# Spatial mixing of a gMLP as seven block products (Strassen) in two sweeps, with the projection as a stage of its own

## The chip, the cores and the metric

The kernel runs on one core of a Trainium2 chip. The metric is the device time of one execution in microseconds (us). Each time given is a median over executions unless a profile is named.

## The reference

Attention (32 heads, the last 512 of 2048 cached positions) gives `s`; a gMLP gives a gate; the output joins them. Cut to what matters:

```python
x  = A_x                                    # 2048 x 512
xn = layernorm(x)
s  = attention(xn) @ wo                     # 2048 x 512
z  = gelu(xn @ w_in)                        # 2048 x 1376
z1 = z[:, :688]
z2 = layernorm(z[:, 688:])                  # 2048 x 688
g  = w_sp @ z2 + b_sp[:, None]              # spatial mixing: 2048x2048 by 2048x688
B  = (z1 * g) @ w_out                       # projection: 688 -> 512
out = x + s * silu(B)
```

Everything is f32.

## The kernel before

**Precision.** TensorE (PE) multiplies here in fp32r, a form of f32 with fewer bits. To keep f32 accuracy each operand is split in two: `hi`, a cast to fp32r on ScalarE (ACT), and `lo`, what is left (`rest`, line 59: `whole - hi`), on VectorE (DVE) or GpSimd (POOL). A product is then three matmuls, hi x hi, hi x lo and lo x hi (`mm3`, lines 65 to 67). So every operand costs an ACT cast and a subtraction before PE can use it.

**Stages.** The program is one instruction stream for each engine, in an order fixed when it is built; nothing is reordered on the chip.

1. *Attention* fills the first 1450 us. In its gaps the first half of z (`z1`, ahead of its gelu) is computed and stored in DRAM (`z1_dram`), and `s` ends up in `s_dram`.
2. *z* (lines 781 to 826): the 16 row tiles of the second half of z, in the order `ZO` (tiles 8 to 15, then 0 to 7). For each: two products of 344 columns into PSUM (`z_product`), gelu on ACT into `z` (`z_gelu`, line 789), statistics and norm on DVE (`z_norm`), and the split into `z2` hi and lo on ACT and POOL (`z_split`, line 807; the last tile's rest on DVE). `z2` then holds all of the normed z, as operands of the right side, 2 x 344 columns for each of 16 chunks of rows.
3. *Mixing and projection* (lines 832 to 994), a loop over the 16 row tiles `i` of `w_sp`:
   - `mix(i)`: 16 chunks x 2 column halves x 3 = 96 matmuls of 344 columns, into the two PSUM banks `ps_g0` and `ps_g1`.
   - `take(4)`: the next row tile of w_sp, in four pieces of 512 columns, is split (ACT cast, line 884; DVE rest), and further pieces of 256 KB are fetched eight pieces ahead on the queue of SyncE (SP).
   - `gate(i)` (line 906, DVE): `u = (g + b_sp) * gelu(z1)` from PSUM, in three instructions; the last 48 columns are written twice so that the projection's sixth chunk can hold hi and lo at once.
   - `send_u(i)`: u must stand transposed for the projection. DVE transposes its 32 x 32 blocks (line 913) into `uB`, and a store to DRAM (`u_dram`) with four loads back puts the blocks in place (`uL`). Only the last tile is transposed on PE (`flip_u`, line 935).
   - `split_u(i-1)` (cast, line 926; two rests on DVE) and `project(i-1)`: 17 matmuls of 512 columns into `ps_f`, silu on ACT, times `s` and plus `x` on DVE (lines 961, 962), and the store to `out`.

So one tile's projection runs behind the next tile's mixing, and the DRAM round trip of u and the splits of w_sp lie beside some 18 us of matmuls each time. The last two tiles are finished in pieces.

Memory: a ring of "x8" buffers, 8 KB per partition each, free after attention, holds w_sp's raw pieces and operands (in the profile all of them are `x`). PSUM has eight banks.

## Time and profile before

| | |
|---|---|
| median of 3 runs | 1812.49 us (1811.61 to 1812.63) |
| span of the profiled execution | 1813.9 us |
| DMA over the span | 394.08 MB, 217 GB/s |

Busy time of each engine by stage (us), in the profiled execution:

| from, to | stage | PE | DVE | ACT | POOL | GB/s |
|---|---|---|---|---|---|---|
| 0 to 1452.5 | attention | 1436.76 | 1242.09 | 1037.57 | 1199.47 | 236 |
| 1452.5 to 1511.5 | z | 59.00 | 34.33 | 26.72 | 33.00 | 67 |
| 1511.5 to 1801 | mixing, projection | 289.50 | 114.68 | 105.55 | 4.78 | 162 |
| 1801 to 1814 | the last tiles | 8.83 | 5.02 | 3.56 | 0.00 | 42 |

The profile is of one execution. A row of a group gives line, engine, operation, output and inputs by the program's names, tile size and count, then the busy time in us, the mean of one in ns, and the idle time ahead of the group with what ended it. A row of the timeline gives the start, the duration (of a group of like instructions, from the first's start to the last's end), the instruction and, in brackets, what it waited for. A row of the windows gives for each engine the busy us and, as x387, the number of instructions, then the granted TensorE clock, the busy share of the DMA engines and their GB/s. PEld is the loading of weights into PE, which overlaps with its matmuls.

### The profile page before, as it was taken

To read this page: it belongs to the slowest core of one execution; us is meant where nothing else is said; L and a number is where in the kernel's file an instruction comes from. 1 tells how busy PE (TensorE), PEld (TensorE's weight loads), DVE (VectorE), ACT (ScalarE), POOL (GpSimd) and SP (SyncE) were. 2 spreads that over 40 slices of the span, in tenths; PEclk is the share of its full clock that TensorE was granted. 3 is DMA by queue.
4 is the path that set the end of the run, shared out by engine and by line. 5 is a ranking of instruction groups with operands and counts; after the bars stand their busy time and mean duration, and the time that the engine had idled before them with its cause. 6 is when DMAs were issued, how large, how long until landed. Compare 5 with 4: busy or idle time off the path is not lost.

```text
span 1813.9 us, 28901 instructions
## 1 busy us (share of the span) xinstructions
PE 1794.1 (99%) x8658; PEld 1541.1 (85%) x8658; DVE 1396.1 (77%) x2369; ACT 1173.4 (65%) x2625; POOL 1237.3 (68%) x1179
## 2 busy tenths in 40 slices
PE   8999999999999999999999999999999999999999
PEld 7888888888888887788888888888888999999998
DVE  5689988989998988788888888888888556433333
ACT  3777777777777776577777777777776444433332
POOL 2798898898888987778888888888887343000000
PEclk8999999999999999999999999999999999999999
DMA  4688887988888989787777777777778725554532
GB/s 168 190 237 239 246 263 228 264 253 231 262 246 244 261 235 294 248 261 222 220 232 223 219 226 224 224 217 231 232 213 268 225 88 170 172 173 146 185 118 93
DMA packets 181805, 394.08 MB, mean 217 GB/s; under 512 B 24368, under 2 KB 54832, under 8 KB 164496
## 3 DMA queue, kind: packets, MB, share of 16 engines
q1 hardware_dynamic: 177040, 386.60, 71.7%
q10 hardware_dynamic: 4608, 5.64, 0.9%
q8 instruction: 68, 1.11, 0.2%
q14 instruction: 89, 0.73, 0.1%
HBM read 225.42 MB, written 166.72 MB: 216 GB/s over the span
## 4 chain that ended last, share of the span: by engine, by line
PE 91%; DVE 3%; DMA 3%; ACT 1%; issue 1%; POOL 1%; SPq 0%; ACTq 0%; DVEq 0%; POOLq 0%
PE ps_a L450 15%; PE ps L67 12%; PE ps L65 12%; PE ps L66 12%; PE ps_a L517 6%; PE ps_a L516 6%; PE ps_a L515 6%; PE ps_g L67 4%; PE ps_g L66 4%; PE ps_g L65 4%; PE ps_a L67 2%; PE ps_a L66 2%; PE ps_a L65 2%; DMA x<-x_dram 1%; PE ps_f L67 1%
## 5 line engine op out<-in xcount | busy, mean ns | idle before, releaser
L59 POOL TENSOR_TENSOR pT_l<-pL,pT_h 128x512 fp32r<-128x512 f32 x507 | 656.5, 1298 | 187.5 <-ACT pT_h L507 169.9
L479 ACT ACTIVATE prob<-ps,nm 128x512 f32<-128x512 f32 x512 | 353.9, 691 | 339.4 <-DVE nm L477 331.7
L539 DVE SCALAR_TENSOR_TENSOR sacc<-ps,sums,sacc 128x512 f32<-128x512 f32 x496 | 370.2, 747 | 128.5 <-PE ps L67 122.8
L450 PE MATMUL ps_a<-x,x 128*128 128x512 f32 x1302 | 376.4, 389 | 4.4 <-DMA x<-x_dram 4.4
L488 DVE STREAM_TRANSPOSE pL<-prob 128x512 f32<-128x512 f32 x512 | 359.2, 702 | 3.0 <-ACT prob L479 3.0
L477 DVE TENSOR_REDUCE nm<-ps 128x1 f32<-128x512 f32 x512 | 340.6, 665 | 6.6 <-PE ps L67 6.5
L507 ACT CAST pT_h<-pL 128x512 fp32r<-128x512 f32 x512 | 318.4, 622 | 20.1 <-DMA pL<-p_dram 7.0
L450 PEld LDWEIGHTS ps_a<-x,x 128*128 128x128 f32 x1302 | 244.5, 188 | 56.5 <-DMA x<-x_dram 4.8
L59 POOL TENSOR_TENSOR wl<-raw,wh 128x512 fp32r<-128x512 f32 x186 | 241.4, 1298 | 13.4 <-ACT wh L144 13.4
L517 PE MATMUL ps_a<-pT_l,wh 128*128 128x512 f32 x512 | 200.4, 391 | 2.0 <-POOL pT_l L59 1.8
L65 PE MATMUL ps<-wh,qT_h 128*128 128x512 f32 x512 | 199.9, 390 | 0.6 <-DVE sacc L539 0.6
L67 PE MATMUL ps<-wh,qT_l 128*128 128x512 f32 x512 | 200.0, 391 | 0.3
L515 PE MATMUL ps_a<-pT_h,wh 128*128 128x512 f32 x512 | 199.9, 391 | 0.0
L65 PE MATMUL ps<-wh,oT_h 128*128 128x512 f32 x512 | 199.7, 390 | 0.0
L66 PE MATMUL ps<-wl,qT_h 128*128 128x512 f32 x512 | 199.5, 390 | 0.0
L67 PE MATMUL ps<-wh,oT_l 128*128 128x512 f32 x512 | 199.5, 390 | 0.0
L516 PE MATMUL ps_a<-pT_h,wl 128*128 128x512 f32 x512 | 199.5, 390 | 0.0
L66 PE MATMUL ps<-wl,oT_h 128*128 128x512 f32 x512 | 199.5, 390 | 0.0
L67 PE MATMUL ps_g<-z_h,x 128*128 128x344 f32 x512 | 161.8, 316 | 0.0
L65 PE MATMUL ps_g<-z_h,x 128*128 128x344 f32 x512 | 161.8, 316 | 0.0
L66 PE MATMUL ps_g<-z_l,x 128*128 128x344 f32 x512 | 161.8, 316 | 0.0
L59 POOL TENSOR_TENSOR x<-wq,x 128x256 fp32r<-128x256 f32 x186 | 138.1, 743 | 1.5 <-ACT x L432 1.5
(197 smaller groups left out, 3184.9 us busy)
## 6 DMA issues: line engine op xcount, KB each, us to landing
p_dram<-pL SPq DMA_DIRECT2D x128, 1024.0 KB, 4.8
pL<-p_dram SPq DMA_DIRECT2D x256, 192.0 KB, 4.0
raw<-wh SPq DMA_DIRECT2D x188, 256.0 KB, 6.2
pL<-p_dram SPq DMA_DIRECT2D x256, 128.0 KB, 4.0
pL<-p_dram SPq DMA_DIRECT2D x256, 64.0 KB, 4.0
wq<-wh SPq DMA_DIRECT2D x62, 256.0 KB, 5.6
x<-w_sp SPq DMA_DIRECT2D x60, 256.0 KB, 5.8
x_dram<-rawx SPq DMA_DIRECT2D x32, 256.0 KB, 5.8
```

The lines of the kernel that those rows point to most:

```text
L59: engine.tensor_tensor(lo, whole, hi.bitcast(F32), op=OP.subtract)
L65: nc.tensor.matmul(ps, lh, rh, start=first, stop=False)
L66: nc.tensor.matmul(ps, lh, rl, start=False, stop=False)
L67: nc.tensor.matmul(ps, ll, rh, start=False, stop=last)
L450: nc.tensor.matmul(qps[g, bank], wt["q", g, k][a][:, c * P:(c + 1) * P], X[g * 2 // H][ORDER[k]][:, b, c], start=first, stop=r == 5, skip_ ...
L477: nc.vector.tensor_reduce(nm, ps, axis=AX.X, op=OP.max, negate=True)
L479: nc.scalar.activation(prob[t], ps, AF.Exp, bias=nm, accum_out=sums[b][:, j:j + 1])
L488: nc.vector.transpose(pL[b][:, :, j * P:j * P + P].rearrange("p a (c q) -> p a c q", q=Q), prob.pop(t).rearrange("p (a c q) -> p a c q", a ...
L507: nc.scalar.copy(h, p)
L515: nc.tensor.matmul(pps[b], vh, ph, start=c == 0, stop=False)
L517: nc.tensor.matmul(pps[b], vh, pl, start=False, stop=c == 3)
L539: nc.vector.scalar_tensor_tensor(at, ps, rs, at, op0=OP.mult, op1=OP.add)
```

## The change

The mixing is the only part whose arithmetic is changed; attention and the products of z stay, and so do the 272 matmuls of the projection.

**Seven products.** w_sp is cut into row tile pairs `r` (tiles r and r + 8) and two halves of its columns, and z into row halves and column halves (344 each). So for a pair there are blocks a11, a12, a21, a22 (128 x 1024 each) and b11, b12, b21, b22. The plain way needs eight block products for a pair; Strassen's scheme, in Winograd's form, needs seven, of sums of blocks:

```
S1 = a21 + a22   S3 = a11 - a21   S2 = S1 - a11   S4 = a12 - S2
T1 = b12 - b11   T3 = b22 - b12   T2 = b22 - T1   T4 = b21 - T2 (sign turned)
P1 = a11 b11  P2 = a12 b21  P3 = S4 b22  P4 = a22 T4  P5 = S1 T1  P6 = S2 T2  P7 = S3 T3
tile r:      P1 + P2                 | P1 + P6 + P5 + P3
tile r + 8:  P1 + P6 + P7 + P4       | P1 + P6 + P7 + P5
```

Each product is a *slot* of 8 chunks x 3 = 24 matmuls of 344 columns: 56 slots, 1344 matmuls, where before there were 16 x 96 = 1536.

**Two sweeps.** The first has 16 slots, P2 and P1 for each pair. For these, `bz` (hi and lo) holds the split left half of z, and the whole z stays as raw f32 in `zr`. From the last tiles of z on DVE forms the T blocks out of `zr` (line 867) and ACT and DVE split them into the operands `tP5`, `tP6`, `tP7` (line 876, line 59); b22 and T4 take the place of b21 and b11 in `bz` at its end (slots 15 and 16, b22's rests on POOL). `evict_1` copies P1 to SBUF on ACT (line 941), stores it in `p1_dram` through ACT's own DMA queue, adds it to P2 on DVE (943), gates the sum with z1 (944) and stores that left half of u in `u0_dram`, again through ACT's queue (945). The second sweep has 40 slots, P6, P5, P7, P3 and P4 for each pair. `load_2` fetches P1 again (`U`, line 962), the left half of u (965) and both tiles' z1 (967, 969), one slot ahead of a pair; for the first pair it stands at slot 17, and its buffers (`pm`) lie where `zr` lay. `evict_2` adds the products' sums on DVE (lines 995, 1001, 1002, 1009 and the sum for P3) and gates them (981); `send_u` transposes u (986) and stores it (988); all of it stays in DRAM (`uD`).

**Operands.** A row tile of w_sp comes in one load of 1 MB (line 808). `a_sum` forms S1, S3, S2 on DVE and S4 on POOL (line 820). `prep(t + 2)` splits the operand of the slot after the next: one ACT cast of 1024 columns (line 832) and one rest of 1024 on DVE (line 59), for P4 on POOL. In the program's order a slot's matmuls come first, then the eviction of the slot before, then `prep`, then the sums and loads that stand in the table `ev` for that slot.

**Projection.** It comes after the last slot, over the 16 tiles in the order 0, 8, 1, 9, ... `load_p` fetches u transposed, s and x three tiles ahead, `split_u` splits the next u behind a tile's matmuls, and `finish_out` is as before. w_out is loaded and split in the last pair's slots (its rests on POOL). No transposes on PE are left.

The core of the diff; what it drops is the loop of stage 3 above:

```diff
-    z2 = (zp.tile([P, NT, 2, ZW], F32R, name="z2_h"), zp.tile([P, NT, 2, ZW], F32R, name="z2_l"))
+    bz = tuple(zp.tile([P, NT, ZW], F32R, name=f"bz_{a}") for a in "hl")
+    zr_stack = ExitStack()
+    zrp = zr_stack.enter_context(tc.tile_pool(name="zrp", bufs=1, side="right", reuse_waits="tile"))
+    zr = zrp.tile([P, NT, 2, NB], F32, name="zr")
...
-        hi, lo = (t[:, i, :, :NB] for t in z2)
-        whole = z[i].rearrange("p (n f) -> p n f", n=2)
-        nc.scalar.copy(hi, whole)
-        rest(engine, lo, whole, hi)
+        hi, lo = (t[:, i, :NB] for t in bz)
+        nc.scalar.copy(hi, zr[:, i, 0])
+        rest(engine, lo, zr[:, i, 0], hi)
...
+    SLOTS = [(r, k) for r in range(RP) for k in ("P2", "P1")] \
+        + [(r, k) for r in range(RP) for k in ("P6", "P5", "P7", "P3", "P4")]
...
+    def a_sum(r, k, engine):
+        a11, a12, a21, a22 = a_blocks(r)
+        if k == 0:
+            s1[r] = x8([P, RP * P], F32)
+        to, x0, x1, op = ((s1[r], a21, a22, OP.add), (a21, a11, a21, OP.subtract),
+                          (a11, s1[r], a11, OP.subtract), (a12, a12, a11, OP.subtract))[k]
+        engine.tensor_tensor(to, x0, x1, op=op)
+    def prep(n, engine):
+        r, k = SLOTS[n]
+        HW = RP * P
+        if k in ("P2", "P1"):
+            src = rows["s", r][:, HW:] if k == "P2" else rows["s", r][:, :HW]
+        else:
+            a11, a12, a21, a22 = a_blocks(r)
+            src = {"P6": a11, "P5": s1[r], "P7": a21, "P3": a12, "P4": a22}[k]
+        op = ops[n] = x8([P, 2, RP, P])
+        hi, lo = (op[:, a].rearrange("p c t -> p (c t)") for a in range(2))
+        nc.scalar.copy(hi, src)
+        rest(engine, lo, src, hi)
...
+    def products(n):
+        r, k = SLOTS[n]
+        first_of = k in ("P2", "P1", "P6", "P5")
+        name = "ps_a" if k in ("P1", "P6", "P7", "P4") else "ps_c"
+        if first_of:
+            bank[r, name] = pp.tile([P, 512], F32, name=name)
+        ps = bank[r, name][:, :NB]
+        op = ops.pop(n)
+        for c in range(RP):
+            rh, rl = operand(k, c)
+            for m, (a, b) in enumerate(((op[:, 0, c], rh), (op[:, 0, c], rl), (op[:, 1, c], rh))):
+                nc.tensor.matmul(ps, a, b, start=first_of and c == 0 and m == 0,
+                                 stop=c == RP - 1 and m == 2, skip_group_check=True)
...
+    def t_diff(j, k):
+        c, d = pair(j)
+        b11, b12, b21, b22 = zr[:, c, 0], zr[:, c, 1], zr[:, d, 0], zr[:, d, 1]
+        if k == "T2":
+            t2[j] = t2_tile[:, j % 2, :, :NB]
+        to, x0, x1 = {"T1": (b11, b12, b11), "T3": (b12, b22, b12), "T2": (t2.get(j), b22, b11),
+                      "T4": (b21, b21, t2.get(j))}[k]
+        nc.vector.tensor_tensor(to, x0, x1, op=OP.subtract)
+    def t_split_z(j, k, engine):
+        c, d = pair(j)
+        src = {"T2": t2.get(j), "T1": zr[:, c, 0], "T3": zr[:, c, 1], "B22": zr[:, d, 1], "T4": zr[:, d, 0]}[k]
+        if k in ("B22", "T4"):
+            hi, lo = (t[:, d if k == "B22" else c, :NB] for t in bz)
+        else:
+            hi, lo = (t[:, c, :NB] for t in tt[{"T2": "P6", "T1": "P5", "T3": "P7"}[k]])
+        nc.scalar.copy(hi, src)
+        rest(engine, lo, src, hi)
...
+    for r in range(RP):
+        on(2 * r - 6 if r else -8, load_rows, ("s", r), r)
+        on(first(r) - 7, load_rows, ("b", r), r + RP)
+        on(first(r) - 6, load_rows, ("a", r), r)
+        for k, (d, e) in enumerate(((-4, V), (-3, V), (-3, V), (-2, G))):
+            on(first(r) + d, a_sum, r, k, e)
+    for j in range(4):
+        on(-4 + 2 * j, t_diff, j, "T1")
+        on(-4 + 2 * j, t_diff, j, "T3")
+        on(3 * j + 1, t_diff, j, "T2")
+        on(3 * j + 1, t_split_z, j, "T2", V)
+        on(3 * j + 2, t_diff, j, "T4")
+        on(3 * j + 2, t_split_z, j, "T1", V)
+        on(3 * j + 3, t_split_z, j, "T3", V)
+        on(15, t_split_z, j, "B22", G)
+        on(16, t_split_z, j, "T4", V)
...
+    def step(t):
+        if 0 <= t + 2 < NS and t + 2 > 1:
+            prep(t + 2, G if SLOTS[t + 2][1] == "P4" else V)
+        for f, args in ev.get(t, ()):
+            f(*args)
...
+    def evict_1(r):
+        p1, z1 = small[:, r % 2], small[:, 2 + r % 3]
+        a, c = (bank.pop((r, n))[:, :NB] for n in ("ps_a", "ps_c"))
+        nc.scalar.copy(p1, a)
+        nc.scalar.dma_start(p1_dram[:, r], p1)
+        nc.vector.tensor_tensor(c, c, p1, op=OP.add)
+        nc.vector.scalar_tensor_tensor(z1, c, bsp[:, r:r + 1], z1, op0=OP.add, op1=OP.mult)
+        nc.scalar.dma_start(u0_dram[:, r], z1)
...
+    def load_2(r):
+        us[r, "U"] = pm.tile([P, NB], F32, name="U", bufs=2)
+        nc.sync.dma_start(us[r, "U"], p1_dram[:, r])
+        us[r, "u"] = pm.tile([P, NF * P], F32, name="u", bufs=4)
+        nc.vector.memset(us[r, "u"][:, FH:], 0.0)
+        nc.sync.dma_start(us[r, "u"][:, :NB], u0_dram[:, r])
+        us[r, "z"] = pm.tile([P, NB], F32, name="z1t", bufs=2)
+        nc.sync.dma_start(us[r, "z"], z1_dram[:, r, NB:])
+        us[r + RP, "z"] = pm.tile([P, FH], F32, name="z1b", bufs=2)
+        nc.sync.dma_start(us[r + RP, "z"], z1_dram[:, r + RP])
...
+    def evict_2(r, k):
+        a, c = (bank[r, n][:, :NB] if (r, n) in bank else None for n in ("ps_a", "ps_c"))
+        U = us[r, "U"]
+        if k == "P6":
+            us[r, "u2"] = pm.tile([P, NB], F32, name="u2", bufs=2)
+            nc.vector.tensor_tensor(us[r, "u2"], a, U, op=OP.add)
+        elif k == "P5":
+            us[r, "p5"] = pm.tile([P, NB], F32, name="p5", bufs=2)
+            nc.scalar.copy(us[r, "p5"], c)
+        elif k == "P7":
+            u3 = pm.tile([P, NB], F32, name="u3", bufs=2)
+            nc.vector.tensor_tensor(u3, a, U, op=OP.add)
+            nc.vector.tensor_tensor(u3, u3, us[r, "p5"], op=OP.add)
+            gate(r + RP, 1, u3)
+        elif k == "P3":
+            nc.vector.tensor_tensor(c, c, us[r, "u2"], op=OP.add)
+            gate(r, 1, c)
+            send_u(r)
+        else:
+            nc.vector.tensor_tensor(a, a, U, op=OP.add)
+            gate(r + RP, 0, a)
+            send_u(r + RP)
+    for r in range(RP):
+        if r:
+            on(first(r) - 1, load_2, r)
+        on(first(r) + 1, gelu_2, r)
+        on(first(r) + 2, gelu_2, r + RP)
...
+    f7 = first(RP - 1)
+    for k in range(NF):
+        on(f7 + 1, load_wo, k)
+        on(f7 + 2 + k // 3, split_wo, k)
+    for n in range(3):
+        on(f7 + 2 + n, load_p, PO[n])
...
+    pm = None
+    for t in range(NS):
+        if t == SWEEP + 1:
+            zr_stack.close()
+            pm = ctx.enter_context(tc.tile_pool(name="pm", bufs=1, side="right", reuse_waits="tile"))
+            load_2(0)
+        products(t)
+        if t == f7:
+            tpool["P6"].close()
+            pw = ctx.enter_context(tc.tile_pool(name="pw", bufs=1, reuse_waits="tile"))
+        if t:
+            r, k = SLOTS[t - 1]
+            if k == "P1":
+                evict_1(r)
+            elif t - 1 >= SWEEP:
+                evict_2(r, k)
+        step(t)
+    evict_2(RP - 1, "P4")
+    for n, i in enumerate(PO):
+        if n == 0:
+            split_u(i)
+        if n + 3 < NT:
+            load_p(PO[n + 3])
+        if n == NT - 1:
+            project(i, 0, D // 2)
+            finish_out(i, 0, D // 2)
+            project(i, D // 2, D)
+            finish_out(i, D // 2, D)
+            continue
+        project(i)
+        split_u(PO[n + 1])
+        finish_out(i)
```

**How the order moves.** On DVE in the mixing of before, this is all that stands there for one row tile: the gates from PSUM (`ps_g`, with `z` the buffer of z1), the transpose, the output of the tile before (`s_t`), the four rests of w_sp's pieces and the two of u (the `x` are w_sp's and u's buffers).

```order
L906 SCALAR_TENSOR_TENSOR u<-ps_g_19167,bsp,z_19001 128x344
L906 SCALAR_TENSOR_TENSOR u<-ps_g_19168,bsp,z_19001 128x344
L906 SCALAR_TENSOR_TENSOR u<-ps_g_19168,bsp,z_19001 128x48
L913 STREAM_TRANSPOSE uB<-u 128x768
L961 TENSOR_TENSOR s_t<-ps_f,s_t 128x512
L962 TENSOR_TENSOR s_t<-s_t,x_t 128x512
L59 TENSOR_TENSOR x_18460<-x_18844,x_18459 128x512 x2
L59 TENSOR_TENSOR x_18460<-x_18845,x_18459 128x512 x2
L59 TENSOR_TENSOR x_18847<-uL,x_18846 128x640
L59 TENSOR_TENSOR x_18846<-uL,x_18846 64x128
```

In the second sweep of after, DVE has this for one row pair from P4 of the pair before (`ps_a` is the PSUM bank, `u` and the `u_` with a number are pieces of u and its sums, `z1b` is z1, `p_20051` is P5, the wide `x` are w_sp's raw blocks, sums and operands).

```order
L1009 TENSOR_TENSOR ps_a<-ps_a,U 128x344
L981 SCALAR_TENSOR_TENSOR u<-ps_a,bsp,z1b 128x344
L986 STREAM_TRANSPOSE uB<-u 128x768
L59 TENSOR_TENSOR x_19991<-x_19736,x_19991 128x1024
L995 TENSOR_TENSOR u_20019<-ps_a,U 128x344
L59 TENSOR_TENSOR x_20021<-x_19771,x_20021 128x1024
L820 TENSOR_TENSOR x_20024<-x_19915 128x1024
L820 TENSOR_TENSOR x_19915<-x_19950,x_19915 128x1024
L820 TENSOR_TENSOR x_19950<-x_20024,x_19950 128x1024
L1001 TENSOR_TENSOR u_20083<-ps_a,U 128x344
L1002 TENSOR_TENSOR u_20083<-u_20083,p_20051 128x344
```

The rests are now 1024 wide, one for each slot that is not P4's; the three sums of the next pair's blocks stand in a row between two evictions.

On ACT in the first sweep of after, these rows are the gelu of z1 (951), the eviction of a pair's P1 (941) with its two stores (942, 945; the buffer `x_18836` holds P1, z1 and u's half) and the casts of w_sp (832) and of T blocks (876) of the slots that follow.

```order
L951 ACTIVATE x_18836<-x_18836 128x344
L941 COPY x_18836<-ps_a 128x344
L942 DMA p_dram<-x_18836 128x344
L945 DMA u_dram<-x_18836 128x344
L832 CAST x_19004<-x_18865 128x1024
L876 CAST tP_h<-x_18835 128x2x344
L832 CAST x_19038<-x_18865 128x1024
L876 CAST tP_h<-zr 128x2x344
```

The store of u's half (945) stands between the eviction and the next cast; before, ACT issued no DMA in this stage.

On SP, after, the stores of the transposed u (988), the 1 MB loads of w_sp (808) and the loads for the next pair (962 to 969) stand like this around the start of a pair.

```order
L808 DMA x_19915<-w_sp 128x2048
L988 DMA u_dram<-uB 128x768
L808 DMA x_19950<-w_sp 128x2048
L962 DMA U<-p_dram 128x344
L965 DMA u<-u_dram 128x344
L967 DMA z1t<-z_dram 128x344
L969 DMA z1b<-z_dram 128x688
L988 DMA u_dram<-uB 128x768
```

The load of P1 (`U`) is issued behind the store of the previous pair's first u and behind w_sp's second megabyte; before, the loads of u followed their store at once, and w_sp came in pieces of 256 KB.

More of the change, by code (lines that the diff above doesn't have):

```diff
@@ L25 @@
 NF = (FH + P - 1) // P
-ZW = 384
+ZW = 352
 EPS = 1e-5
@@ new lines, in pair @@
+    def pair(j):
+        return slice(2 * j, 2 * j + 2), slice(RP + 2 * j, RP + 2 * j + 2)
+    def t_diff(j, k):
[6 more added lines that the diff above has]
+        nc.vector.tensor_tensor(to, x0, x1, op=OP.subtract)
@@ new lines, in mixer_kernel @@
+    f7 = first(RP - 1)
+    for k in range(NF):
+        on(f7 + 1, load_wo, k)
[18 more added lines that the diff above has]
+                evict_2(r, k)
+        step(t)
```

279 lines of the change are left out of this document (113 added, 166 removed).

## The prediction

> **What bounds the kernel now.** I read the page first, then the busy time by stage, then the matmuls in order of time inside the mixing stage, then the groups of that stage.
>
> ```profile
> span 1813.9 us, 28901 instructions
> PE 1794.1 (99%) x8658; PEld 1541.1 (85%) x8658; DVE 1396.1 (77%) x2369; ACT 1173.4 (65%) x2625; POOL 1237.3 (68%) x1179
> ...
> 1452.50:1511.50 59.00, 59.00 (x387) 59.00 (x386) 34.33 (x61) 26.72 (x50) 33.00 (x31) 1.00 0.19 67
> 1511.50:1801.00 289.50, 289.50 (x1776) 280.22 (x1775) 114.68 (x191) 105.55 (x143) 4.78 (x5) 1.00 0.51 162
> ```
>
> From 1452.5 us (z) to 1801.0 us (mixing and projection) PE never stops; DVE is busy 114.7 of the 289.5 us of mixing, POOL 4.8. So here only matmuls cost time, and the other engines have room. A matmul's own span overlaps the next one's, so I price it by the distance of starts:
>
> ```profile
> 1600.56 0.32 PE L65 MATMUL ps_g<-z_h,x 128*128 128x344 f32 x1
> ...
> 1615.13 0.32 PE L67 MATMUL ps_g<-z_h,x 128*128 128x344 f32 x1
> 1615.28 0.39 PE L65 MATMUL ps_f<-wo_h,x 128*128 128x512 f32 x1
> ...
> 1619.13 0.32 PE L65 MATMUL ps_g<-z_h,x 128*128 128x344 f32 x1
> ```
>
> These are the 96 matmuls of one row tile's mixing: 14.57 us over 95 distances, 0.1534 us each. The 17 of its projection take 1619.13 - 1615.28 = 3.85 us.
>
> **What is removed.** Mixing falls from 16 x 96 = 1536 to 56 x 24 = 1344 matmuls of the same shape: 192 x 0.1534 = **-29.4 us**. The last tile's six PE transposes go too; their spans are
>
> ```profile
> 1801.02 0.38 PE L935 MATMUL ps_u<-ident,u 128*128 128x128 f32 x2
> ...
> 1803.31 0.60 PE L935 MATMUL ps_u<-ident,u 128*128 128x128 f32 x4
> ```
>
> and overlap the next matmul: **-0.5**. The projection keeps its matmuls. Everything else is cost, and the question is whether DVE, ACT and the loads can feed a PE that now takes 24 x 0.1534 = 3.68 us per product ("slot"). Their prices:
>
> ```profile
> L59 DVE TENSOR_TENSOR x<-x,x 128x512 fp32r<-128x512 f32 x61 | 38.0, 685 | 15.4 <-ACT x L884 15.4
> L906 DVE SCALAR_TENSOR_TENSOR u<-ps_g,bsp,z 128x344 f32<-128x344 f32 x31 | 16.5, 572 | 106.6 <-PE ps_g L67 106.6
> L913 DVE STREAM_TRANSPOSE uB<-u 128x768 f32<-128x768 f32 x15 | 14.7, 979 | 0.5
> L926 ACT CAST x<-uL 128x768 fp32r<-128x768 f32 x15 | 12.5, 835 | 9.4 <-DMA uL<-u_dram 9.1 <-issue 0.2
> L59 DVE TENSOR_TENSOR x<-uL,x 128x640 fp32r<-128x640 f32 x15 | 12.3, 819 | 5.5 <-ACT x L926 5.4
> L884 ACT CAST x<-x 128x512 fp32r<-128x512 f32 x61 | 33.4, 613 | 0.3 <-DMA x<-w_sp 0.2
> ...
> 1603.97 2.50 DVE L59 TENSOR_TENSOR x<-x,x 128x512 fp32r<-128x512 f32 x4 [1.18 <-ACT x L884]
> ```
>
> On DVE, 512 columns take 685 ns and 640 take 819: 1.05 ns a column, so 1024 take 1.22 us and 688 take 0.87. Four in line take 2.50 us, (2.50 - 0.69) / 3 = 0.60 each instead of 0.69, so one that need not wait costs 0.08 less: 1.14 and 0.79. A 344-wide gate or addition is 0.5 to 0.6. An ACT cast of 1024 is 835 + 256 x 0.87 = 1.06 us.
>
> **Second sweep, per row pair (5 slots, 18.4 us of PE).** DVE does four operand rests and three sums of w_sp's blocks, 7 x 1.14 = 8.0; eight 344-wide additions and gates at 0.55, 4.4; two 48-wide gates 0.4; two transposes 2.0; memsets 0.1: **14.9 us**. That fits. What doesn't show in it is POOL, which before did almost nothing here and now has a rest and a sum of 1024 columns per pair. Where POOL and DVE worked on SBUF together, the trace has this:
>
> ```profile
> 1514.06 1.68 POOL L59 TENSOR_TENSOR z_l<-z,z_h 128x688 fp32r<-128x688 f32 x1
> ...
> 1517.05 1.68 POOL L59 TENSOR_TENSOR z_l<-z,z_h 128x688 fp32r<-128x688 f32 x1 [1.31 <-ACT z_h L807]
> ...
> 1517.67 1.79 DVE L59 TENSOR_TENSOR z_l<-z,z_h 128x688 fp32r<-128x688 f32 x1 [1.01 <-ACT z_h L807]
> ...
> L59 POOL TENSOR_TENSOR x<-raw_z,x 128x512 fp32r<-128x512 f32 x4 | 5.2, 1288 | 0.0
> ```
>
> DVE's rest of 688 columns should take 0.87 us and took 1.79: it ended 0.73 us after POOL's (1519.46 against 1518.73), as if it had waited for all of it. POOL takes 1288 ns for 512 columns and 1.68 us for 688, 2.2 ns a column, 2.4 us for 1024. So up to 4.8 us of a row's DVE time can be lost. I take 4.3, because DVE's work between the two POOL instructions is two-input SBUF work in the order shown, all but one addition from PSUM (0.5).
>
> The Trainium skill, page "SBUF — State Buffer", section "Who interferes with whom", says that it is an exclusive lock which a two-input DVE instruction and a POOL instruction that reads SBUF contend for, and that whichever issues first holds it to its end. The row above shows the one side of this; no row here has POOL waiting for DVE. If DVE mostly came first, POOL would wait instead and those 4.3 us would go, which is the first rival below.
>
> Third, the load of U (p1 of the pair) stands on SP behind the store of the transposed u and a 1 MB load of w_sp, and DVE's next eviction waits for it.
>
> ```profile
> x<-w_sp SPq DMA_DIRECT2D x60, 256.0 KB, 5.8
> u_dram<-uB SPq DMA_DIRECT2D x15, 384.0 KB, 2.3
> ...
> z<-z_dram SPq DMA_DIRECT2D x16, 344.0 KB, 4.6
> ...
> DMA to landing us min/median/max: 2.1/3.5/4.8
> ```
>
> Counted from the end of that transpose, DVE has a rest (1.14), an eviction with its transpose (2.1) and a rest (1.14) to do, 4.4 us. U is issued after two other issues, at about 0.9; with 5 us to land (between z's 4.6 behind 256 KB and w_sp's 5.8; the last row, s_t's, bounds it below at 2.1) it is there at 5.9: DVE waits **1.5** (0 to 2.3). The row comes to 14.9 + 4.3 + 1.5 = 20.7 us against 18.4: **2.3 us lost per row pair** (0 to 3.6), six rows, 13.8.
>
> **First sweep (16 slots, 58.9 us of PE).** Every eviction is now a chain over two engines: ACT copies P1, DVE adds and gates, ACT issues the store of the result and only then casts the next operand, and DVE's rest waits for that cast. DVE is free of z about 5.4 us after the sweep starts (its last z rest ended 7.9 us after mixing began; z's splits are half as wide now). Up to slot 16's rest it then has 15 rests, 17.1; twelve sum-or-rest instructions of 688 at 0.79, eight dependent ones at 0.87, four more differences, 19.8; seven evictions at 1.15, 8.0; three block sums, 3.6: 48.5 us. It waits 1.5 us per eviction (store issue 0.33, cast 1.06, hand-over 0.1), 10.5, and 0.86 for each of four T2 casts, 3.4. 5.4 + 48.5 + 13.9 = 67.8 against slot 16's third matmul at 59.2: **8.6 late** (5 to 11). The issue is priced by
>
> ```profile
> L362 ACTq DMA_DIRECT2D z_dram<-z x16: 326/326/345, 1392.3 to 1453.3; - x16
> ```
>
> **Between the sweeps (slots 16 to 21).** DVE's work to slot 21's rest: four rests 4.6, four T4 rests 3.2, an eviction 1.15, P6's addition 0.55, three sums 3.6, P7's eviction 1.95: 15.1. Waits: the four B22 rests on POOL are 6.7 us, of which I let half fall on DVE's two-input work (3); ACT's four B22 casts stand ahead of slot 18's cast (3); U of the first pair can't be issued before the last T4 rest, since the new tiles lie where z lay, and needs 2.1 at the least; the pair's own POOL work 4.3. Together 27.5, so slot 21's rest is at 95.3, PE could take it at 77.7: 17.6, **9.0 more** (4 to 13).
>
> **Start of the sweep.** The first product takes the PSUM bank that z's last gelu still reads.
>
> ```profile
> 1511.39 0.32 PE L67 MATMUL ps_a<-raw,x 128*128 128x344 f32 x1
> 1511.55 0.32 PE L65 MATMUL ps_g<-z_h,x 128*128 128x344 f32 x1
> ...
> 1511.75 0.46 ACT L789 ACTIVATE z<-ps_a 128x344 f32<-128x344 f32 x1 [1.32 <-PE ps_a L67]
> ```
>
> Before, mixing went on at 1511.55; now it waits for 1511.75 + 0.46: **+0.7**.
>
> **Hand-over to the projection.** Nothing of PE's work covers the last eviction any more: DVE adds, gates and transposes P4 (2.1) before the rest of the first u (0.82), and PE has two matmuls (0.45) meanwhile: **+2.6**. Such a wait has a second price:
>
> ```profile
> 28.50 0.66 PE L202 MATMUL ps<-ident,sacc 128*128 128x128 f32 x4 [1.93 <-DVE sacc L193]
> ...
> 30.02 0.49 PE L66 MATMUL ps_a<-wl,x 128*128 128x344 f32 x1
> 30.30 0.49 PE L67 MATMUL ps_a<-wh,x 128*128 128x344 f32 x1
> ```
>
> After a wait of 1.93 us matmuls of 344 columns stood 0.28 us apart, half rate, up to 32.3 us: some 3.5 us, so 1.7 lost. **+1.7** at the hand-over; in the sweeps PE's slack against DVE takes it up. The Trainium skill ("TensorE: Matmul & The Clock Gate", "What's actually happening") has the clock fall after an idle window of about 3.4 us; the row shows it after less. By the page's rule the 1.7 would go and the sum be 1819.
>
> **Projection stage.** 16 x 3.85 us of PE. Per tile 1152 KB are loaded or stored; the stage's 162 GB/s at 0.51 busy makes some 318 GB/s the most, 3.7 us: about PE's own pace, so a load comes late now and then: **+2** (0 to 5). Silu and gelu no longer alternate, but their table loads were covered by PE anyway.
>
> **Sum.** -29.4 - 0.5 + 0.7 + 8.6 + 9.0 + 13.8 + 2.6 + 1.7 + 2 = +8.5. The profiled span is 1813.9 us, the median of the three runs 1812.5; the difference carried to the median gives **1821 us**. What a measurement here can tell from no change is about 0.2%, 3.6 us.
>
> **Rivals.**
> 1. *The second sweep keeps PE's pace.* POOL's two instructions fall beside DVE's PSUM work (evictions and transposes, 6.9 us a row), and U lands in time; a row then needs 14.9 of 18.4 us. For it: no row shows POOL winning against a queue of DVE work. Left are 0.7, 8.6, some 5 between the sweeps and 2.6: -29.9 + 16.9 = -13, **1800**. Chance 0.25.
> 2. *Losses and gain cancel.* Half of the port's and U's waits are hidden: 2.3 becomes 0.6 per row and 9 becomes 6, and the clock and the projection cost 1 together: -29.9 + 0.7 + 8.6 + 6 + 3.6 + 2.6 + 1 = -7 at the one end, the forecast less 5 at the other, around **1812**. Chance 0.17.
> 3. *The clock decides.* PE waits once per row at P6's operand, about 2.3 us, near the 1.93 that halved the rate. If each such fall isn't taken up by DVE's lateness, seven rows and three places of the first sweep cost 10 x 1.7 = 17 more: **1838**. It decides where PE after a wait is later than DVE's next operand. Chance 0.10.
> 4. *The matmuls are all that counts.* Operands are prepared two slots ahead; if that covers the chains, -29.9 + 0.7 + 2.6 = **1786**. Against it: DVE's sums above. Chance 0.04.
>
> The forecast keeps 0.44 (its own range 1814 to 1832). Faster by over 0.2%: rivals 1 and 4, 0.29. Within 0.2%: 0.17. Slower: 0.54. The range must leave out at most 2 in 10: without rival 4, half of 3 and the tails, 1798 to 1835.
>
> **What would show it.** In the changed profile: PE busy about 30 us less, with idle time put down to DVE rests (L59) in both sweeps, DVE near 90% busy there; L59 rests of 1024 columns at 1.2 us alone and up to 3.6 beside POOL; P6's addition (L995) waiting for U's load; the sweeps together about 237 us after their start instead of 206. I am wrong if PE's distance between slots stays 3.68 us in the second sweep, or if the lost time is in the loads of w_sp.

## The result, and the profile after

The changed kernel takes 1827.68 us (median of 4 runs, 1824.3 to 1828.54), the kernel before 1812.31 us beside it: a ratio of 1.0080, 95% interval 1.0066 to 1.0094, slower by 15 us. The forecast was 1821 us, 1798 to 1835.

The page of the changed kernel, in the lines that answer to those of before, then its busy time by stage: z, the first sweep (slots 0 to 15), slots 16 to 20, the other seven pairs of the second sweep, the projection. The columns are as before; the last three are the granted TensorE clock, the DMA share and GB/s.

```profile
span 1822.5 us, 28703 instructions
PE 1778.2 (98%) x8460; PEld 1516.2 (83%) x8460; DVE 1516.3 (83%) x2468; ACT 1174.9 (64%) x2632; POOL 1287.3 (71%) x1203
...
1448.85:1508.43 59.58, 59.04 (x386) 58.76 (x384) 33.95 (x63) 23.11 (x50) 23.77 (x29) 1.00 0.33 118
1508.43:1575.70 67.27, 63.23 (x385) 60.36 (x385) 51.09 (x63) 29.73 (x45) 5.08 (x5) 1.00 0.49 165
1575.70:1604.88 29.18, 21.26 (x120) 20.73 (x121) 23.05 (x25) 13.39 (x19) 12.98 (x7) 0.88 0.36 118
1604.88:1750.63 145.75, 135.35 (x843) 133.47 (x841) 124.37 (x144) 47.83 (x61) 44.54 (x20) 0.99 0.53 179
1750.63:1822.52 71.89, 64.65 (x291) 51.25 (x289) 42.15 (x69) 23.18 (x33) 0.90 (x1) 0.99 0.87 257
```

PE is busy 16 us less, not 30, and waits in every stretch behind z; DVE has 120 us more work than before. The two profiled executions may be compared only from z on. Before, z began at 1452.67 us (1448.85 after), because that execution of before ran more of its first 46 us at half the clock (a granted clock of 0.89 there, 0.96 in the changed kernel's):

```profile
0.00:46.28 46.28, 37.73 (x200) 34.87 (x201) 25.33 (x59) 17.33 (x45) 10.71 (x22) 0.89 0.50 169
46.28:1452.67 1406.39, 1399.20 (x6246) 1159.32 (x6244) 1216.89 (x2049) 1020.24 (x2382) 1188.76 (x1122) 1.00 0.81 238
1452.67:1511.55 58.88, 58.88 (x387) 58.88 (x385) 34.20 (x60) 26.72 (x50) 33.00 (x31) 1.00 0.19 66
1511.55:1813.92 302.37, 298.28 (x1833) 288.00 (x1831) 119.70 (x202) 109.11 (x149) 4.78 (x5) 1.00 0.49 157
```

From z's first product to the end it is 361.25 us before and 373.67 after: 12.4 us more. By stage, against 24 x 0.1534 us per slot: the start of the first sweep +0.7, its 16 slots 67.27 instead of 58.9 (+8.4), slots 16 to 20 29.18 instead of 18.4 (+10.8), seven pairs 145.75 instead of 128.8 (+17.0), the hand-over 2.5, the projection some 3, against -29.9 of removed matmuls. The remaining 3 us to the medians' 15.4 fit the clock, though no profile of those executions shows it: the profiled execution had a mean granted clock of 0.995, the other three 0.992 to 0.993. A stretch at half rate lasts 3.41 us here, or twice that, and each 3.41 us lower the mean by 0.5 x 3.41 / 1825 = 0.0009, so they would have had two or three more, at up to 1.7 us each.

Where PE waits in the second sweep, the timeline of PE shows (the first matmuls of slots: P7 of pair 0, then P7, P3 and P4 of pair 3, then P7 of pair 4; pairs are counted from 0):

```profile
1591.67 0.62 PE L853 MATMUL ps_a<-tP_h,x 128*128 128x344 f32 x1 [7.24 <-DVE u L995]
...
1655.29 0.39 PE L853 MATMUL ps_a<-tP_h,x 128*128 128x344 f32 x1 [2.17 <-DVE u L995]
...
1659.13 0.32 PE L853 MATMUL ps_c<-bz_h,x 128*128 128x344 f32 x1
...
1662.91 0.32 PE L853 MATMUL ps_a<-bz_h,x 128*128 128x344 f32 x1
...
1676.83 0.40 PE L853 MATMUL ps_a<-tP_h,x 128*128 128x344 f32 x1 [2.38 <-DVE u L995]
```

Two things are to be seen. From slot 18 to the end of the sweep each wait that PE's timeline names is that of P7 for L995, P6's addition, which reads the PSUM bank that P7 adds to. And a slot without any wait (P3, 1659.13 to 1662.91) takes 3.78 us, 0.1575 a matmul, not 3.68. DVE, POOL and SP around 1655.29:

```profile
1650.98 1.18 DVE L59 TENSOR_TENSOR x<-x,x 128x1024 fp32r<-128x1024 f32 x1
1654.63 0.52 DVE L995 TENSOR_TENSOR u<-ps_a,U 128x344 f32<-128x344 f32 x1 [2.46 <-DMA U<-p_dram]
...
1657.44 4.56 DVE L820 TENSOR_TENSOR x<-x,x 128x1024 f32<-128x1024 f32 x2
...
1657.44 3.47 POOL L59 TENSOR_TENSOR x<-x,x 128x1024 fp32r<-128x1024 f32 x1 [14.22 <-DVE x L820]
...
1647.85 0.32 SPq L988 DMA_DIRECT2D u_dram<-uB  x1
1648.26 0.38 SPq L808 DMA_DIRECT2D x<-w_sp  x1
1648.69 0.47 SPq L962 DMA_DIRECT2D U<-p_dram  x1
```

DVE stands 2.46 us until U has landed, 5.9 us after its issue behind the store and the megabyte. At 1657.44 two sums that take some 1.2 us each when alone take 4.56 beside POOL's rest.

### The profile page after: what moved, and what is told of

Same layout as the page of the kernel before. It is cut to its first block, busy times and chain, and to the rows that moved or that the text cites. A ratio compares the mean times of both kernels' runs of the same rounds, so it can differ in the third digit from the quotient of the medians.

```text
span 1822.5 us, 28703 instructions
## 1 busy us (share of the span) xinstructions
PE 1778.2 (98%) x8460; PEld 1516.2 (83%) x8460; DVE 1516.3 (83%) x2468; ACT 1174.9 (64%) x2632; POOL 1287.3 (71%) x1203
## 4 chain that ended last, share of the span: by engine, by line
PE 74%; DVE 12%; DMA 7%; ACT 3%; issue 2%; SPq 1%; POOL 1%; ACTq 0%; DVEq 0%; POOLq 0%
PE ps_a L450 15%; PE ps L67 12%; PE ps L65 12%; PE ps L66 12%; PE ps_a L517 6%; PE ps_a L515 6%; PE ps_a L516 6%; DVE x L820 2%; DMA U<-p_dram 2%; DVE x L59 2%; PE ps_a L65 2%; PE ps_a L66 2%; PE ps_a L67 2%; DMA x<-u_dram 1%; DMA p_dram<-pL 1%
## 5 line engine op out<-in xcount | busy, mean ns | idle before, releaser
L59 POOL TENSOR_TENSOR pT_l<-pL,pT_h 128x512 fp32r<-128x512 f32 x507 | 657.4, 1300 | 186.0 <-ACT pT_h L507 181.1
L507 ACT CAST pT_h<-pL 128x512 fp32r<-128x512 f32 x512 | 318.5, 622 | 18.4 <-DMA x<-x_dram 6.7
L59 POOL TENSOR_TENSOR wl<-raw,wh 128x512 fp32r<-128x512 f32 x186 | 241.7, 1299 | 13.4 <-ACT wh L144 13.4
L59 POOL TENSOR_TENSOR x<-wq,x 128x256 fp32r<-128x256 f32 x186 | 138.5, 745 | 1.5 <-ACT x L432 1.5
L144 ACT CAST wh<-raw 128x512 fp32r<-128x512 f32 x188 | 117.9, 627 | 2.0 <-issue 1.1
L517 PEld LDWEIGHTS ps_a<-pT_l,wh 128*128 128x128 f32 x512 | 96.2, 188 | 24.4 <-POOL pT_l L59 4.7
L67 PEld LDWEIGHTS ps<-wh,qT_l 128*128 128x128 f32 x512 | 96.3, 188 | 22.0 <-DVE qT_l L59 2.0
```

Source lines behind the costliest of these rows:

```text
L59: engine.tensor_tensor(lo, whole, hi.bitcast(F32), op=OP.subtract)
L67: nc.tensor.matmul(ps, ll, rh, start=False, stop=last)
L507: nc.scalar.copy(h, p)
L517: nc.tensor.matmul(pps[b], vh, pl, start=False, stop=c == 3)
```

## The experiments

The theory to be tested: the second sweep loses its time through U's late load, with POOL's lock behind it, the first through the order of ACT's queue, the stretch between through the splits; and, new, the matmuls themselves are dearer in the sweeps. The main rivals: DVE's work as such sets the pace, or the clock does. "Before" stands for the runs of the kernel before beside each.

**1. Only the spacing of z in SBUF, in the kernel before.**

```diff
-ZW = 384
+ZW = 352
```

> The kernel before, with one number changed: z2's rows of chunks are 352 words apart instead of 384, as in the changed kernel; nothing else moves. In the changed kernel matmuls of the sweeps stand 0.1574 us apart instead of 0.1533. Theory (where the moving operand lies in SBUF costs it): the 1536 mixing matmuls go to 0.157 to 0.158 us each, 1536 x 0.004 = 6.3 us more, and since PE never waits here all of it shows: 1818 to 1819 us. Rival (the longer distance comes from 24 matmuls in a row into one PSUM bank, or from more traffic of other engines): the distance stays 0.1533 and the time 1812.3 us.

Measured: 1817.03 us against 1812.05, ratio 1.0027 (1.0018 to 1.0037). First and last of the 96 mixing matmuls of a row tile, on PE's timeline of this kernel:

```profile
1597.26 0.32 PE L65 MATMUL ps_g<-z_h,x 128*128 128x344 f32 x1
...
1612.15 0.32 PE L67 MATMUL ps_g<-z_h,x 128*128 128x344 f32 x1
```

14.89 us over 95 distances are 0.1567 each, where it was 0.1534: 1536 x 0.0033 = 5.1 us, which is what the time shows. The same instructions in the same order on the same engines: the place of z alone does it. The time is a little less than the expected 1818 to 1819; the rival is out.

**2. U loaded two slots earlier.**

```diff
-            on(first(r) - 1, load_2, r)
+            on(first(r) - 3, load_2, r)
```

> The changed kernel with load_2 of every pair but the first two slots earlier, so that P1 (U) is asked for before the transposed u and the megabyte of w_sp. Theory (in the second sweep U's landing is what PE waits for, through DVE's addition for P6 that frees the PSUM bank for P7): that wait of 2.0 to 2.5 us per pair goes, pairs fall from 20.8 us in the mean to about 19.1, seven of them 11 to 12 us, and with the waits two or three half-rate stretches of 1.7 us: 1811 to 1816 us. Rival (DVE's 18.9 us of work per pair, 4 of it lost to POOL's lock on SBUF, sets the pace): the wait moves to the operand rests, pairs stay above 20.3 us, and the time above 1823 us.

Measured: 1811.01 us against 1812.05, ratio 0.9992 (0.9981 to 1.0002), so 16.7 below the changed kernel: the whole loss of 15 us is gone with one number. Seven pairs, by the windows, and the group of P6's additions on DVE:

```profile
1606.93:1738.90 131.97, 131.97 (x842) 131.97 (x841) 110.91 (x143) 47.28 (x61) 39.03 (x20) 1.00 0.59 196
...
L995 DVE TENSOR_TENSOR u<-ps_a,U 128x344 f32<-128x344 f32 x7 | 3.6, 512 | 0.0
```

PE is busy all of 131.97 us, 18.85 a pair, PE's own pace; no addition waits for U. That is 13.8 us less than 145.75; the rest of the 16.7 may be the clock, which is 1.00 in these pairs, but that is not shown.

**3. POOL's two instructions per pair given to DVE.**

```diff
-        for k, (d, e) in enumerate(((-4, V), (-3, V), (-3, V), (-2, G))):
+        for k, (d, e) in enumerate(((-4, V), (-3, V), (-3, V), (-2, V))):
...
-            prep(t + 2, G if SLOTS[t + 2][1] == "P4" else V)
+            prep(t + 2, V)
```

> The changed kernel with POOL's work of the second sweep, P4's rest and the sum S4, given to DVE; U's load stays where it was. Theory (both waits are one: the lock makes DVE's eviction of P3 late, hence the transposed u, hence U's issue behind it): DVE's row falls from 18.9 to some 17.3 us, U is issued about 3 us earlier against the products, and the wait goes though nothing of the load is changed: 1812 to 1818 us. Rival (U's distance to landing alone sets it): pairs stay at 20.8 us and the time at 1825 to 1828 us. Second rival (DVE is full, 2.4 us more work per pair make it the bound): above 1828 us.

Measured: 1818.63 us, just above the expected 1812 to 1818, ratio 1.0037 (1.0024 to 1.0050). The sums and P7's second addition on DVE, with P6's, in the changed kernel and in this one:

```profile
L820 DVE TENSOR_TENSOR x<-x,x 128x1024 f32<-128x1024 f32 x12 | 27.1, 2262 | 0.4
L1002 DVE TENSOR_TENSOR u<-u,p 128x344 f32<-128x344 f32 x7 | 15.6, 2222 | 0.7
L995 DVE TENSOR_TENSOR u<-ps_a,U 128x344 f32<-128x344 f32 x7 | 3.6, 514 | 15.4 <-DMA U<-p_dram 15.4
```

```profile
L820 DVE TENSOR_TENSOR x<-x,x 128x1024 f32<-128x1024 f32 x12 | 14.7, 1222 | 0.2
L1002 DVE TENSOR_TENSOR u<-u,p 128x344 f32<-128x344 f32 x7 | 4.4, 623 | 0.2
L995 DVE TENSOR_TENSOR u<-ps_a,U 128x344 f32<-128x344 f32 x7 | 3.6, 515 | 16.4 <-DMA U<-p_dram 16.4
```

The lock is real: it cost (27.1 - 14.7) + (15.6 - 4.4) = 23.6 us in seven pairs, 3.4 a pair. Without it the seven pairs take 137.5 us instead of 145.75: three of them 18.85, four 19.6 to 20.6. So the two losses hang together, as I held, but not all is won (8.2 us of the early load's 13.8 in these pairs): DVE still stands 16.4 us for U, because U's issue stays behind u's store.

**4. Both.**

> Both edits: U's load two slots earlier, and no work on POOL in the second sweep. Theory: PE's own pace, 5 x 3.78 = 18.9 us per pair, with no wait; not more than 2 us below the better of the two alone, since each takes away the same wait: 1810 to 1814 us. Rival (the two losses add up): 10 us or more below the better of the two.

Measured: 1812.99 us, ratio 1.0004 (0.9993 to 1.0014), all seven pairs 18.85 us, as with the early load alone. The two do not add up: with U in time, the lock lies within DVE's slack.

**5. First sweep: the store behind the cast.**

```diff
         nc.vector.scalar_tensor_tensor(z1, c, bsp[:, r:r + 1], z1, op0=OP.add, op1=OP.mult)
-        nc.scalar.dma_start(u0_dram[:, r], z1)
...
             prep(t + 2, G if SLOTS[t + 2][1] == "P4" else V)
+        if t > 0 and SLOTS[t - 1][1] == "P1":
+            r = SLOTS[t - 1][0]
+            nc.scalar.dma_start(u0_dram[:, r], small[:, 2 + r % 3])
```

> The changed kernel with one instruction moved: ACT issues the store of u's left half behind the cast of the next operand, not ahead of it; nothing else. Theory (in the first sweep each eviction stops DVE for 1.5 us, because its next rest waits for a cast that stands on ACT behind that store, which waits for DVE's own gate): the stop falls to about 0.5 us, eight times, and the 16 slots go from 67.3 us to 61 to 63 (PE alone takes 60.5), so 1822 to 1824 us against 1827.7. Rival (the sums and splits on DVE are too long by themselves): the stop only moves, and the sweep stays above 65 us.

Measured: 1820.48 us, a little better than expected, ratio 1.0041 (1.0026 to 1.0057). An eviction and the next rest, on DVE and ACT, in the changed kernel:

```profile
1539.90 0.58 DVE L944 SCALAR_TENSOR_TENSOR x<-ps_c,bsp,x 128x344 f32<-128x344 f32 x1
1541.95 1.23 DVE L59 TENSOR_TENSOR x<-x,x 128x1024 fp32r<-128x1024 f32 x1 [1.48 <-ACT x L832]
...
1540.50 0.33 ACTq L945 DMA_DIRECT2D u_dram<-x  x1
1540.87 1.05 ACT L832 CAST x<-x 128x1024 fp32r<-128x1024 f32 x1 [2.89 <-DVE x L944]
```

and in this one (the gate is L947, the store L907 here):

```profile
1541.33 0.58 DVE L947 SCALAR_TENSOR_TENSOR x<-ps_c,bsp,x 128x344 f32<-128x344 f32 x1
1541.82 1.21 DVE L59 TENSOR_TENSOR x<-x,x 128x1024 fp32r<-128x1024 f32 x1
...
1539.81 1.05 ACT L832 CAST x<-x 128x1024 fp32r<-128x1024 f32 x1 [0.40 <-ACT x L944]
1541.94 0.33 ACTq L907 DMA_DIRECT2D u_dram<-x  x1
```

The cast now runs beside the eviction, DVE's stop of 1.48 us is gone, and the 16 slots take 61.3 us instead of 67.3, against PE's 60.5. The theory holds.

**6. Three edits of order**: 2, 5, and the first split of u ahead of the last eviction.

```diff
+    split_u(PO[0])
     evict_2(RP - 1, "P4")
     for n, i in enumerate(PO):
-        if n == 0:
-            split_u(i)
```

> The changed kernel with three edits of order: U loaded two slots earlier, the store of u's left half behind the cast, and the split of the first u ahead of the last eviction, so that the projection need not wait for that. Theory: from the 1811.0 us of the early load, 4 to 6 off in the first sweep and 2.6 at the hand-over to the projection: 1803 to 1805 us, ahead of the kernel before by 7 to 9 us. Rival (what is won in the first sweep is lost again between the sweeps, where DVE and POOL still have all splits of b22 and T4 to do before z's place is free): slots 16 to 20 grow by what the first sweep loses, 1808 to 1809 us.

Measured: 1802.84 us against 1812.60, ratio 0.9941 (0.9927 to 0.9955): as expected, and ahead of the kernel before. Slots 16 to 20 take 28.0 us, so the rival is out; from the projection's first matmul to the end it is 68.1 us instead of 71.9, with no wait at its start.

**7. P1 of the first pair kept in SBUF.** It goes to unused words behind T2's buffer, and `load_2(0)` no longer fetches it.

> The three edits, and P1 of the first pair kept in SBUF, in unused words of T2's buffer, instead of stored and loaded again after z's place is free. Theory: slot 18 then waits only for DVE to come through the four rests of T4, not for a load behind them: the wait of 7.2 us there shrinks by 2.2 to 2.6 us and, being shorter, may lose the half-rate stretch behind it (1.7 to 3.4 us): 3 to 5 us below the three edits. Rival (the first pair's z1, loaded at the same place, is then what comes late): less than 1 us.

Measured: 1801.96 us, ratio 0.9941 (0.9927 to 0.9955): no difference that these runs can tell. The wait of slot 18 fell from 6.9 us in kernel 6 to 5.2, less than expected; P6's addition still stands behind T4's four rests on DVE. The 3 to 5 us of the theory did not come. The rival's size did (under 1 us), but not its mechanism: PE has no wait behind slot 18's in these sweeps, so z1 doesn't come late.

**8. The place of a matmul's operands, by itself.** A loop over groups of 48 matmuls, in place of the kernel.

> Not the reference's computation: it leaves out all but 22 groups of 48 matmuls of 344 columns, each with its moving operand at another offset (0, 128, 256, 384, 512, 32, 96, 224, 352, 480, 0 bytes against the place that the operands of before have within 512), first with the weights at that same place, then with them 128 bytes further. Theory (the moving operand's place within 512 bytes sets the distance): 0.1533 us at offsets 0 and 512, 0.155 to 0.160 at the others, whatever the weights' place. Rival (what counts is whether weights and moving operand lie alike): in the second half offset 128 has the 0.1533 and offset 0 has not.

Measured: one profile. Three of the groups (with two or three matmuls of the group ahead): moving operand at offset 0 with the weights at place 0, at 128 with the weights at 128, and at 32 with the weights at 128:

```profile
84.02 8.20 PE L57 MATMUL p<-moving,held 128*128 128x344 f32 x51
...
99.14 7.84 PE L57 MATMUL p<-moving,held 128*128 128x344 f32 x50
...
128.80 8.31 PE L57 MATMUL p<-moving,held 128*128 128x344 f32 x51
```

The last matmul's own span is 0.32, so these are (8.20 - 0.32) / 50 = 0.1576, 0.1535 and 0.1598 us. Both theories fall: with the weights at 0 none of the eleven groups has 0.1533 (0.1556 to 0.158 but for the first, which starts slower), with the weights at 128 only the offsets 128 and 384 have it. At a granted clock of 1.00, the place of both operands counts, between 0.1533 and 0.1600; by which rule stays open.

**9. P7 in a PSUM bank of its own**, in the changed kernel.

```diff
-        first_of = k in ("P2", "P1", "P6", "P5")
-        name = "ps_a" if k in ("P1", "P6", "P7", "P4") else "ps_c"
+        first_of = k in ("P2", "P1", "P6", "P5", "P7")
+        name = {"P7": "ps_b", "P4": "ps_b", "P1": "ps_a", "P6": "ps_a"}.get(k, "ps_c")
...
-            nc.vector.tensor_tensor(u3, a, U, op=OP.add)
+            nc.vector.tensor_tensor(u3, b, us[r, "u2"], op=OP.add)
...
-            nc.vector.tensor_tensor(a, a, U, op=OP.add)
+            nc.vector.tensor_tensor(b, b, us[r, "u2"], op=OP.add)
```

> The changed kernel with P7 (and P4 behind it) in a PSUM bank of its own; its evictions add u2 = P6 + U in place of U, so no operation is added. P7 need no longer wait for P6's eviction; U's load stays late. Theory (DVE, which works in order, is what stands still for U, 2.5 us of a pair, and has 18.9 us of work): the wait moves from P7's first matmul to the rests behind it, pairs stay at 20 to 21 us and the time at 1822 to 1828 us. Rival (PE waits for the bank alone): pairs fall to 18.85 us as with the early load, 1811 us.

Measured: 1828.56 us, just above the expected 1822 to 1828, ratio 1.0085 (1.0072 to 1.0098). P6's additions in seven pairs:

```profile
L995 DVE TENSOR_TENSOR u<-ps_a,U 128x344 f32<-128x344 f32 x7 | 3.6, 516 | 17.5 <-DMA U<-p_dram 17.5
```

DVE stands for U as long as ever. PE now waits about 2 us at P4, for P7's eviction, instead of at P7; the pairs take 20.7 to 24.2 us but for the last. The bank named in the wait was not the cause; DVE, which stands for U ahead of all its later work, was.

**10. T4's rests one slot later**, behind P6's eviction and P3's rest, in kernel 7; the first pair's P6 sum and P5 copy lie in free words of `small`, and z1 of the pair is asked for first.

```diff
-        on(16, t_split_z, j, "T4", V)
+        on(17, t_split_z, j, "T4", V)
...
-        if t == SWEEP + 1:
+        if t == SWEEP + 2:
```

> The three edits, P1 of the first pair kept, and the rests of T4 one slot later, behind P6's eviction and the rest for P3; to allow that, P6's sum and P5's copy of the first pair lie in free words of another buffer, and the buffers that take z's place are opened a slot later. Theory (slots 16 to 20 lose their 7.8 us because four rests of T4 stand on DVE ahead of P6's eviction): P7 starts without a wait, the five slots go from 26.7 us to 20 to 21, the half-rate stretch goes too: 1795 to 1797 us. Rival (z1 of the first pair, loaded a slot later now, takes its place: DVE stands at P7's gate and P6 of the second pair waits): 24 us or more, 1800 us.

Measured: 1800.74 us, ratio 0.9940 (0.9925 to 0.9954), slots 16 to 20 26.2 us. These are the rival's sizes. P7 waits only 0.4 us, as expected, but P4 waits 4.0, and my theory that the order of T4 was the loss falls:

```profile
1594.49 0.39 PE L853 MATMUL ps_a<-bz_h,x 128*128 128x344 f32 x1 [4.01 <-DVE u L1006]
...
1585.84 5.42 DVE L59 TENSOR_TENSOR bz_l<-zr,bz_h 128x688 fp32r<-128x688 f32 x4
```

P7's eviction (L1006) stands behind T4's rests and two sums on DVE instead. It isn't z1 either, as the rival had it: the gate on DVE doesn't wait for it. DVE has more work there than five slots hold: it is busy 22.1 us, and PE needs 18.9. Behind the wait of 4.0 us slot 20 ran at half rate in part, 5.39 us.

**11. PE kept busy** in kernel 6, ahead of slot 18 (the bank is one of the projection's).

```diff
+        if t == SWEEP + 2:
+            idle = pp.tile([P, 512], F32, name="ps_f")
+            for n in range(40):
+                w = tt["P5"][0][:, 0]
+                nc.tensor.matmul(idle[:, :NB], w[:, :P], w[:, :NB], start=n == 0, stop=n == 39)
         products(t)
```

> The three edits, and 40 matmuls more, whose sums nobody reads, ahead of slot 18's, where PE waited for 7.2 us: 40 x 0.157 = 6.3 us. Theory (PE's standing still lowers the granted clock, and the slot behind the wait runs its first matmuls at half rate, 5.72 us instead of 3.78): slot 18 takes 3.8 us, and the time falls by 1.9 us to 1801 us though there is more work. Rival (the clock falls at times of its own): slot 18 or its neighbours stay at 5 us or more, 1803 us.

Measured: 1800.60 us, ratio 0.9930 (0.9916 to 0.9945); the interval overlaps that of kernel 6, so the time alone doesn't settle it. PE's timeline does; slot 18 and the start of slot 19 in kernel 6:

```profile
1585.68 0.63 PE L853 MATMUL ps_a<-tP_h,x 128*128 128x344 f32 x1 [6.89 <-DVE u L997]
...
1591.40 0.32 PE L853 MATMUL ps_c<-bz_h,x 128*128 128x344 f32 x1
```

and here, with the 40 matmuls ahead:

```profile
1577.97 6.47 PE L1096 MATMUL ps_f<-tP_h 128*128 128x344 f32 x40
1585.10 0.39 PE L853 MATMUL ps_a<-tP_h,x 128*128 128x344 f32 x1 [0.66 <-DVE u L997]
...
1588.94 0.32 PE L853 MATMUL ps_c<-bz_h,x 128*128 128x344 f32 x1
```

Slot 18 takes 1588.94 - 1585.10 = 3.84 us, where it took 5.72 in kernel 6: no half rate, where PE didn't stand still. In all eight profiles in which PE stood still for over 5 us in slots 16 to 20, the clock fell. Of the 1.9 us little is left in the five slots, 27.3 us instead of 28.0: P6's addition came some 1.1 us later against the start of slot 16.

**12. No POOL work in the sweeps**, on top of kernel 10, with 14 such matmuls ahead of slot 20.

```diff
-        on(15, t_split_z, j, "B22", G)
+        on(15, t_split_z, j, "B22", V)
```

and the two lines of experiment 3.

> The kernel with T4's rests one slot later, with two additions: all of POOL's work in the sweeps (b22's four rests, P4's rests, S4) is done by DVE, and 14 matmuls more, whose sums nobody reads, stand ahead of slot 20's, where PE still waited for 4.0 us. Theory (DVE's work sets the pace of slots 16 to 20, and POOL's lock is 6.4 us of it: four DVE instructions there take 2.2 to 2.6 us instead of 0.5 to 1.2 and two sums 4.6 instead of 2.4): DVE gets 5.6 us of new work and is rid of 6.4, so the five slots go from 26.2 us to 24 to 25.5, without a half-rate stretch: 1797 to 1799 us, the fastest of all. Rival (new work of DVE is not paid back by the lock): 27 us or more, 1801 to 1803 us.

Measured: 1797.13 us against 1811.42, ratio 0.9910 (0.9897 to 0.9924), the fastest of all. T4's four rests on DVE, and slots 16 to 20:

```profile
1585.33 3.22 DVE L59 TENSOR_TENSOR bz_l<-zr,bz_h 128x688 fp32r<-128x688 f32 x4
...
1574.13:1596.69 22.56, 21.47 (x136) 20.98 (x135) 21.32 (x29) 12.70 (x18) 0.00 (x0) 1.00 0.57 193
```

Four rests take 3.22 us instead of 5.42, the five slots 22.6 instead of 26.2, better than expected, at a granted clock of 1.00. PE's own 18.9 are not reached: DVE is busy 21.3 of the 22.6. The two edits aren't told apart: slot 20 takes 3.86 us instead of 5.39, so 1.5 of the 3.6 us are the half rate that is gone, and that can be owed to the 14 matmuls or to a shorter wait.

## Why the prediction was right, and where its sum was short

The sign and the mechanism hold; the sum was 8.5 us and came to 15.4. By its own steps:

- *Removed matmuls, -29.4.* The step that failed: the 1344 matmuls that stay were priced at 0.1534 us as "of the same shape". They stand 0.1574 apart in the changed kernel, 5.5 us in all. The diff has two changes of place, the narrower spacing `ZW` (352 words instead of 384) and a dropped tile `gap`; experiment 1 puts 3.3 ns a matmul on the spacing alone. That the missing pad adds the rest is not shown.
- *Start of the sweep, +0.7*: 59.58 us for z instead of 58.88, +0.7.
- *First sweep, +8.6*: +8.4, of which 1.6 is the distance and 6.8 the chain over DVE and ACT. The stop of 1.5 us per eviction was there at 1.48, and experiment 5 took it away.
- *Slots 16 to 20, +9.0*: +10.8, with B22 and T4 in the way, U behind them, and, not foreseen there, a half-rate stretch. That DVE's work is the limit, 10 and 12 bear out.
- *Second sweep, 2.3 in each of six rows, +13.8*: +17.0, of it 3.2 the distance. That the rest equals the forecast is in part luck, since the parts were off against each other: the lock is 3.4 a pair, not 4.3, and DVE's wait for U 2.2 (15.4 / 7), not 1.5. The mechanism, both added to DVE's work, holds. But the first rival's condition, U landing in time, was one number away, and gave PE's pace in all seven pairs (experiment 2); that kernel takes 1811 us and not the rival's 1800, since the distance (5.5) and slots 16 to 20 (29.7 us there) stay.
- *Hand-over, +2.6* (its own terms, 2.1 + 0.82 - 0.45, give 2.5): a wait of 2.48 us of the projection's third matmul for DVE; gone in experiment 6.
- *Half rate, +1.7*: not at the hand-over in the profiled execution, but at 1591.67 and 1676.83 (the slots took 5.64 and 5.41 us). In the profiles of 2 to 5 and 9, with a like wait at the hand-over, it came there too. By the mean clocks the other executions had two or three more; if so, the third rival, that the clock decides, is worth some 3 us beyond the profile.
- *Projection, +2*: some +3, of it 0.5 us at each of three tiles, which wait for the split of u; the rest is not resolved.
- *The signs*: PE's idle time in the second sweep stands behind P6's addition and not behind the rests (L59); DVE is busy 76 to 85% in the sweeps and not near 90; the sweeps take 242 us, 237 were forecast.

The lock was cited from the Trainium skill ("SBUF — State Buffer", "Who interferes with whom"), where the instruction that comes first holds the port. The trace of the changed kernel agrees, and shows the side that no row of before had: at 1657.44 POOL's rest and DVE's two sums start together, POOL takes 3.47 us instead of the 2.42 it takes at 1594.88, about DVE's first sum more, and DVE's second sum then waits for POOL, 4.56 us for both instead of 2.4. On the clock, the Trainium skill ("TensorE: Matmul & The Clock Gate", "What's actually happening") has a window of about 3.4 us that runs freely; the trace agrees in the length, 3.41 us, and in that like waits end differently: after 2.17 us at 1655.29 slot 33 kept its rate (3.84 us), after 2.38 at 1676.83 slot 38 didn't. The trace's clock records say why. The half-rate stretches of the changed kernel begin at 25.51, 728.66, 1588.82 and 1677.56, which are 206, 252 and 26 times 3.413 us apart. On that grid the wait of 2.38 us lies within one window (1674.15 to 1677.56), while a boundary at 1653.67 cuts the one of 2.17 into 0.55 and 1.62, and one at 1752.65 cuts the hand-over's 2.48 into 1.40 and 1.09. So PE need not stand idle for all of a window, as the prediction's row of before, with 1.93 us, had it too.

Not tried: the spacing of 384 words in the changed kernel. Its operands would need 32 x 4 x (2 x 16 + 6 x 8) = 10240 bytes more of each partition; whether there is room, no run shows.

## What to carry to other kernels

Fewer matmuls pay only as far as the other engines and the loads keep the faster pace, so ask of each wait which instruction stands ahead of the late one in its queue: here one number in a table of events, which put a small load behind a megabyte and behind a store that depends on DVE, was worth 16 us of a kernel whose arithmetic saving is 29. A bank or an engine that a wait names may only be the last link; giving P7 its own bank moved the wait by two slots and saved nothing. And a diff that narrows a spacing in memory is to be priced like one that changes instructions.

## What the runs showed of the hardware

The distance of matmuls of one shape, at full clock and with nothing else different, went from 0.1533 to 0.1600 us with the place of the moving operand and the weights in SBUF. PE's clock is halved for 3.41 us or a multiple, beginning on a grid of 3.413 us. From z on, in the 13 profiles (all but experiment 8's), it fell behind every full-rate window of the grid in which PE's rows leave 1.87 us or more free, and behind none with 1.76 or less (of two between, behind one; the last window of a run is left out). So what a wait costs depends on where it falls. With 40 matmuls for nobody in a wait of 7 us it didn't fall, and the time was no longer. And giving POOL's work to DVE, the fuller engine, made DVE's stretch shorter: four rests fell from 5.42 to 3.22 us.
